# A grouped 1x1 convolution over 262144 pixels: two shared pieces in place of the 32-row piece

## The chip, the cores and the metric

The kernel runs on one core of a Trainium2 chip. The metric is the device time of one execution in microseconds; lower is better. The core has 16 DMA engines, which all of its transfers share.

## The reference

```python
# x: (1, 512, 512, 192) bf16, w: (1, 1, 4, 48, 48) bf16; G = 4 groups of Cg = 48 channels, k = 1
xg = xp.reshape(B, H, W, G, Cg)
out = out + jnp.einsum('bhwgc,gcd->bhwgd', xg, w[0, 0])
return out.reshape(B, H, W, C)
```

Every pixel's 192 channels are four groups of 48, and each group is multiplied by a 48 x 48 matrix of its own. All of x (100.66 MB) is read once, and an output of the same size is written.

## The kernel before, in words

**Layout.** A ring in SBUF, `ring`, has 128 rows (partitions) of 520 columns; a column is one pixel of 192 bf16 values, 384 bytes, in each row. It is divided into 5 places of 104 columns. A *piece* is a stretch of pixels that is loaded into one place, computed in the place (the output overwrites the input) and stored from it. A full piece of n columns takes 128 x n consecutive pixels, n to a row.

**Order.** `plan_pieces` lays the pieces out in *slots*, 0 to 20; slot s lies in place s mod 5. Slot 0 holds the head, three small pieces of 8, 20 and 32 columns. Nineteen slots hold a full piece of 104 columns (`BIG`). Slot 10 holds the *32-row piece* (`NARROW`): 48 columns, but only in rows 0 to 15 and 32 to 47. Its two blocks of 16 rows are transfers whose DRAM side is written with an outer dimension of 4 (`transfers`, lines 107 to 115), and each runs on four DMA engines, four rows on each; a full piece runs on all 16, eight rows on each. Pixels: 128 x (60 + 19 x 104) + 32 x 48 = 262144.

**Loads** are issued by SyncE (queue q1 of the profile), in the order of the pieces (line 175). Before it loads slot s it waits until all stores of slot s - 5 have landed.

**Compute** goes by *groups* of four columns, 521 in all: 15 in the head, 26 in a full piece, 12 in the 32-row piece, which takes as long per group as a full one. Two groups are a pair. TensorE transposes a group's 128 x 768 values in six 128 x 128 blocks (line 203) into PSUM, VectorE copies a pair to SBUF (line 242), TensorE multiplies by the weights (line 218), and ScalarE copies the result from PSUM into the ring (line 260). TensorE waits for a piece's load at that piece's first group. The semaphore `fa_done` counts ScalarE's copies.

**Stores** are issued by ScalarE (queue q10), between its copies, as soon as the copies of a piece, or of a part of it, are counted in `fa_done` (line 254). The pieces of slots 15 to 19 are stored in two halves of 52 columns (`LATE_PARTS`), the last in parts of 32, 32, 24 and 16 columns (`LAST_PARTS`).

GpSimd builds two constant tiles in the first 2 us and then does nothing more.

Of the kernel before, what the change touches and what calls it, by code (L numbers as in the profile page):

```python
# [6 lines left out]
BF16 = mybir.dt.bfloat16  # L7
# [4 lines left out]
C = GROUPS * CG  # L12
# [11 lines left out]

BIG = 104
RCOLS = 5 * BIG
HEAD = (8, 20, 32)
LATE = 6
LATE_PARTS = (52, 52)
LAST_PARTS = (32, 32, 24, 16)  # L30
FULL = ((0, 128),)
NARROW = ((0, 16), (32, 16))
NARROW_COLS = 48
NARROW_AT = (9,)
NXP = 4
NXS = 3
NOB = 4
# [2 lines left out]
class Waiter:  # L40

    def __init__(self, eng):
        self.eng = eng
        self.seen = {}
# [5 lines left out]
        self.eng.wait_ge(sem, val)  # L50


class Piece:

    def __init__(self, i, slot, at, g0, size, blocks, pix):
        self.i, self.slot, self.at, self.size = i, slot, at, size
        self.g0, self.g1 = g0, g0 + size // 4
        self.full = blocks is FULL
        self.blocks = []
        for (r0, rows) in blocks:  # L60
            self.blocks.append((r0, rows, pix))
            pix += rows * size
        self.pix_end = pix
        assert size % 4 == 0 and self.at + size <= RCOLS


def plan_pieces(npix):
    few = NARROW_COLS * sum(rows for _, rows in NARROW)
    at = [i for i in NARROW_AT if npix >= len(NARROW_AT) * few + 128 * (sum(HEAD) + BIG * (i + 2))]
    cols = (npix - few * len(at)) // 128  # L70
    assert cols % 4 == 0
    head = list(HEAD) if cols >= sum(HEAD) + BIG else []
    mid = cols - sum(head)
    slots = [[(BIG, FULL)]] * (mid // BIG) + ([[(mid % BIG, FULL)]] if mid % BIG else [])
    for i in at:
        slots.insert(i, [(NARROW_COLS, NARROW)])
    if head:
        slots.insert(0, [(s, FULL) for s in head])
    pieces, g, pix = [], 0, 0
    for n, parts in enumerate(slots):  # L80
        c = n * BIG % RCOLS
        for s, blocks in parts:
            pieces.append(Piece(len(pieces), n, c, g, s, blocks, pix))
            c, g, pix = c + s, pieces[-1].g1, pieces[-1].pix_end
    assert pix == npix
    return pieces


def bass_standalone__grouped__vision_kernel(nc, x, w, out):
    B, H, W_, Cx = x.shape  # L90
    assert Cx == C and tuple(w.shape) == (1, 1, GROUPS, CG, CG)
    npix = B * H * W_
    assert npix % 512 == 0, "the pixel count must be a multiple of 512"

    pieces = plan_pieces(npix)
# [4 lines left out]
    xf = x.rearrange("b h w c -> (b h w) c")  # L100
    of = out.rearrange("b h w c -> (b h w) c")
# [2 lines left out]
    def groups(pair):  # L104
        return range(2 * pair, min(2 * pair + 2, NG))

    def transfers(ap, ring, p, c0=0, c1=None):
        c1 = c1 or p.size
        for (r0, rows, pix) in p.blocks:
            px = ap[pix:pix + rows * p.size, :]  # L110
            if p.full:
                view = px.rearrange("(p i) n -> p (i n)", p=rows)[:, c0 * C:c1 * C]
            else:
                view = px.rearrange("(c a i) n -> a c (i n)", a=4, c=rows // 4)
            yield view, ring[r0:r0 + rows, (p.at + c0) * C:(p.at + c1) * C]

    stores = []
    for p in pieces:
        late = pieces[-1].slot - p.slot
        parts = LAST_PARTS if late == 0 else LATE_PARTS if late < LATE else (BIG,)  # L120
        c = 0
        for n in parts if p.size == BIG and p.full else (p.size,):
            stores.append((p, c, c + n, p.g0 + (c + n) // 4))
            c += n
    st_val = {p: 16 * sum(len(p.blocks) for q, *_ in stores if q is p) for p in pieces}

    with ExitStack() as es:
        block = es.enter_context(nc.Block())
# [9 lines left out]
        def sem(name):  # L138
            return es.enter_context(nc.semaphore(name))

        ld_sem = [sem(f"ld{p.i}") for p in pieces]
        st_sem = [sem(f"st{p.i}") for p in pieces]
        w_sem, id_sem, e_sem, wb_sem, wc_sem = (sem(s) for s in ("w_sem", "id_sem", "e_sem", "wb_sem", "wc_sem"))
        p0_sem, p1_sem = sem("p0_sem"), sem("p1_sem")
        t_done, mm_done = sem("t_done"), sem("mm_done")
        e_done, fa_done = sem("e_done"), sem("fa_done")

        def columns(g):
            p = piece_of[g]
            at = p.at + 4 * (g - p.g0)  # L150
            return ring[:, at * C:(at + 4) * C]

        @block.gpsimd
        def _(gp):
            gp.memset(esel[:], 1.0).then_inc(p0_sem, 1)  # L155
            gp.memset(ident[:], 1.0).then_inc(p1_sem, 1)  # L156
            gp.wait_ge(p0_sem, 1)
            gp.affine_select(out=esel[:], in_=esel[:], pattern=[[-1, ECOLS]],  # L158
                             compare_op=AluOpType.is_equal, fill=0.0, base=ESHIFT,
                             channel_multiplier=1).then_inc(e_sem, 1)  # L160
            gp.wait_ge(p1_sem, 1)
            gp.affine_select(out=ident[:], in_=ident[:], pattern=[[-1, 128]],  # L162
                             compare_op=AluOpType.is_equal, fill=0.0, base=0,
                             channel_multiplier=1).then_inc(id_sem, 1)

        @block.sync
        def _(sp):
            wq = Waiter(sp)
            sp.dma_start(w_sb[:], wv).then_inc(w_sem, 16)  # L169
            for p in pieces:  # L170
                for q in pieces:
                    if q.slot == p.slot - RCOLS // BIG:
                        wq.wait(st_sem[q.i], st_val[q])
                for dram, sbuf in transfers(xf, ring, p):
                    sp.dma_start(sbuf, dram).then_inc(ld_sem[p.i], 16)  # L175

        @block.tensor
        def _(pe):
            wq = Waiter(pe)

            def build_weights():
                wq.wait(e_sem, 1)
                wq.wait(w_sem, 16)
                last = None
                for (tc, r, g, c0_) in WBLOCKS:
                    s0 = ESHIFT - r
                    col = WOFF[tc] + c0_
                    last = pe.matmul(o_ps[:, NOB - 1, col:col + CG], lhsT=esel[:, s0:s0 + 128],  # L188
                                     rhs=w_sb[:, g, :], start=True, stop=True, skip_group_check=True)
                last.then_inc(wb_sem, 1)  # L190

            def transposes(pair):
                wq.wait(e_done, pair - 1)
                last = None
                for g in groups(pair):
                    p = piece_of[g]
                    if g == p.g0:
                        wq.wait(ld_sem[p.i], 16 * len(p.blocks))
                    xg = columns(g)
                    for ul in range(2):  # L200
                        for tc in range(3):
                            j = ul * 3 + tc
                            last = pe.transpose(xT_ps[:, g % NXP, j * 128:(j + 1) * 128],  # L203
                                                xg[:, j * 128:(j + 1) * 128], ident[:])
                last.then_inc(t_done, 1)

            def matmuls(pair):
                wq.wait(e_done, pair + 1)
                for g in groups(pair):
                    xs = xT_sb[pair % NXS][:, g % 2 * 2 * UC:(g % 2 + 1) * 2 * UC]  # L210
                    wq.wait(fa_done, g - 1)
                    last = None
                    for ul in range(2):
                        v = 2 * g + ul
                        for tc in range(3):
                            j = ul * 3 + tc
                            c0_, c1_ = COLR[tc]
                            last = pe.matmul(o_ps[:, v % NOB, c0_:c1_], lhsT=xs[:, j * 128:(j + 1) * 128],  # L218
                                             rhs=wt[:, WOFF[tc]:WOFF[tc] + (c1_ - c0_)],
                                             start=(tc == 0), stop=(tc == 2), skip_group_check=True)  # L220
                    last.then_inc(mm_done, 1)

            build_weights()
            wq.wait(id_sem, 1)
            transposes(0)
            wq.wait(wc_sem, 1)
            for pair in range(NP):
                if pair + 1 < NP:
                    transposes(pair + 1)
                matmuls(pair)  # L230
# [14 lines left out]
        @block.scalar  # L245
        def _(act):
            wq = Waiter(act)
            todo = list(stores)

            def store():  # L250
                p, c0, c1, g1 = todo.pop(0)
                wq.wait(fa_done, g1)
                for dram, sbuf in transfers(of, ring, p, c0, c1):
                    act.dma_start(dram, sbuf).then_inc(st_sem[p.i], 16)  # L254

            for g in range(NG):
                wq.wait(mm_done, g + 1)
                v = 2 * g
                dst = columns(g).rearrange("p (u c) -> p u c", u=2)
                act.copy(dst, o_ps[:, v % NOB:v % NOB + 2, 0:UC]).then_inc(fa_done, 1)  # L260
                while todo and todo[0][3] <= g:
                    store()
            while todo:
                store()
            for p in pieces:
                wq.wait(st_sem[p.i], st_val[p])
# [28 lines left out]
```

## Time and profile before

| | |
|---|---|
| runs | 485.15, 485.40, 485.44 us, median 485.4 |
| span of the profiled execution, first to last instruction | 483.3 us, 2.1 us under the median; its time with what lies around the span isn't listed separately |
| mean granted TensorE clock | 0.961 |
| moved by DMA | 202.23 MB in 7834 packets, mean 418 GB/s |
| TensorE waiting for loads | 21.1 us, 8 waits |
| SyncE's queue waiting for stores to land | 342.7 us in 15 waits, and 56.1 in one |
| issues | 25 loads of the ring and weights by SyncE, 32 stores by ScalarE, none by GpSimd |

How to read it: the page gives busy times of the compute engines, a row on the DMA engines by 40 slices of the span (the mean over the 16), and a part on the DMA queues. A queue isn't an engine: each transfer of q1 or q10 is spread over up to 16 engines, and every engine serves the packets of all queues. A packet is one row of a piece here, 39936 bytes for 104 columns; after its last row of a transfer an engine writes a semaphore, a packet of 4 bytes. q8 and q14 carry instructions that the core's engines fetch while they run, in packets of 16384 and 8192 bytes.

### The profile page before, as it was taken

To read this page: it belongs to the slowest core of one execution; us is meant where nothing else is said; L and a number is where in the kernel's file an instruction comes from. 1 tells how busy PE (TensorE), PEld (TensorE's weight loads), DVE (VectorE), ACT (ScalarE), POOL (GpSimd) and SP (SyncE) were. 2 spreads that over 40 slices of the span, in tenths; PEclk is the share of its full clock that TensorE was granted. 3 is DMA by queue.
4 is the path that set the end of the run, shared out by engine and by line. 5 is a ranking of instruction groups with operands and counts; after the bars stand their busy time and mean duration, and the time that the engine had idled before them with its cause. 6 is when DMAs were issued, how large, how long until landed. Compare 5 with 4: busy or idle time off the path is not lost.

```text
span 483.3 us, 13933 instructions
## 1 busy us (share of the span) xinstructions
PE 431.3 (89%) x6262; PEld 392.1 (81%) x6262; DVE 250.2 (52%) x262; ACT 392.6 (81%) x522; POOL 1.3 (0%) x8
## 2 busy tenths in 40 slices
PE   5699999999999999998599999979998999999910
PEld 5599888898898889887588988969787898899800
DVE  2345655656555565564256555544554655556500
ACT  2669999999999999998299999877888999999920
POOL 1000000000000000000000000000000000000000
PEclk9979999999999999999799999998999999999965
DMA  8999999999999999999999999999999999999993
GB/s 351 431 406 421 449 425 421 422 424 442 434 428 419 425 420 439 425 434 424 431 434 437 424 431 428 432 431 426 434 428 428 430 424 422 439 416 427 429 390 156
DMA packets 7834, 202.23 MB, mean 418 GB/s; under 512 B 1056, under 2 KB 1056, under 8 KB 1696
## 3 DMA queue, kind: packets, MB, share of 16 engines
q10 hardware_dynamic: 4360, 100.67, 48.7%
q1 hardware_dynamic: 3416, 100.68, 48.7%
q8 instruction: 50, 0.82, 0.6%
q14 instruction: 8, 0.07, 0.0%
HBM read 100.68 MB, written 100.66 MB: 417 GB/s over the span
## 4 chain that ended last, share of the span: by engine, by line
PE 54%; DMA 39%; ACT 1%; issue 1%; SPq 0%; ACTq 0%
PE o_ps L218 31%; PE xT_ps L203 22%; DMA ring<-in_x_dram 20%; DMA out_dram<-ring 19%; ACT ring L260 1%; SPq L175 0%; ACTq L254 0%; SPq L169 0%
## 5 line engine op out<-in xcount | busy, mean ns | idle before, releaser
L260 ACT CAST ring<-o_ps 128x768 bf16<-128x768 f32 x521 | 391.3, 802 | 68.5 <-PE o_ps L218 61.0
L242 DVE COPY xT_sb<-xT_ps 128x1536 bf16<-128x1536 bf16 (+1 forms) x261 | 249.6, 956 | 206.0 <-PE xT_ps L203 206.0
L218 PE MATMUL o_ps<-wt,xT_sb 128*128 128x144 bf16 (+1 forms) x3126 | 292.0, 236 | 5.9 <-ACT ring L260 1.3
L218 PEld LDWEIGHTS o_ps<-wt,xT_sb 128*128 128x128 bf16 x3126 | 212.0, 99 | 43.4 <-ACT ring L260 30.2
L203 PE MATMUL xT_ps<-ident,ring 128*128 128x128 bf16 x3126 | 222.7, 221 | 21.1 <-DMA ring<-in_x_dram 21.1
L203 PEld LDWEIGHTS xT_ps<-ident,ring 128*128 128x128 bf16 x3126 | 191.1, 99 | 22.7 <-DMA ring<-in_x_dram 19.8
L188 PE MATMUL o_ps<-w_sb,esel 48*128 48x48 bf16 x10 | 0.6, 210 | 2.7 <-DMA w_sb<-in_w_dram 2.7
L188 PEld LDWEIGHTS o_ps<-w_sb,esel 48*128 48x128 bf16 x10 | 0.5, 113 | 2.6 <-POOL esel L158 2.6
L236 DVE CAST wt<-o_ps 128x480 bf16<-128x480 f32 x1 | 0.7, 658 | 3.3 <-PE o_ps L188 3.3
L260 ACT ACT_TABLE_LOAD x1 | 1.3, 1283 | 0.8 <-PEq L280 0.8
L158 POOL TENSOR_SCALAR_AFFINE_SELECT esel<-esel 48x272 bf16<-48x272 bf16 x1 | 0.4, 405 | 0.0
L155 POOL MEMSET esel<- 48x272 bf16 x1 | 0.3, 318 | 0.3 <-POOLq L280 0.3
L162 POOL TENSOR_SCALAR_AFFINE_SELECT ident<-ident 128x128 bf16<-128x128 bf16 x1 | 0.3, 285 | 0.0
L156 POOL MEMSET ident<- 128x128 bf16 x1 | 0.2, 198 | 0.0
L280 POOL MEMSET const-bfloat16-1.0<- 128x1 bf16 x1 | 0.1, 102 | 0.0
L280 POOL MEMSET const-uint8-127<- 128x1 uint8 x1 | 0.1, 102 | 0.0
L280 POOL MEMSET const-float32-0.0<- 128x1 f32 x1 | 0.1, 98 | 0.3 <-issue 0.3
L280 POOL MEMSET const-float32-1.0<- 128x1 f32 x1 | 0.1, 98 | 0.0
## 6 DMA issues: line engine op xcount, KB each, us to landing
ring<-in_x_dram SPq DMA_DIRECT2D x19, 4992.0 KB, 37.5
out_dram<-ring ACTq DMA_DIRECT2D x13, 4992.0 KB, 45.5
out_dram<-ring ACTq DMA_DIRECT2D x10, 2496.0 KB, 47.7
out_dram<-ring ACTq DMA_DIRECT2D x3, 1536.0 KB, 19.7
ring<-in_x_dram SPq DMA_DIRECT2D x1, 1536.0 KB, 8.4
out_dram<-ring ACTq DMA_DIRECT2D x1, 1152.0 KB, 16.6
ring<-in_x_dram SPq DMA_DIRECT2D x1, 960.0 KB, 5.2
out_dram<-ring ACTq DMA_DIRECT2D x1, 960.0 KB, 28.6
```

The source lines that it names most:

```text
L155: gp.memset(esel[:], 1.0).then_inc(p0_sem, 1)
L156: gp.memset(ident[:], 1.0).then_inc(p1_sem, 1)
L158: gp.affine_select(out=esel[:], in_=esel[:], pattern=[[-1, ECOLS]], compare_op=AluOpType.is_equal, fill=0.0, base=ESHIFT, channel_multipli ...
L162: gp.affine_select(out=ident[:], in_=ident[:], pattern=[[-1, 128]], compare_op=AluOpType.is_equal, fill=0.0, base=0, channel_multiplier=1) ...
L188: last = pe.matmul(o_ps[:, NOB - 1, col:col + CG], lhsT=esel[:, s0:s0 + 128], rhs=w_sb[:, g, :], start=True, stop=True, skip_group_check=True)
L203: last = pe.transpose(xT_ps[:, g % NXP, j * 128:(j + 1) * 128], xg[:, j * 128:(j + 1) * 128], ident[:])
L218: last = pe.matmul(o_ps[:, v % NOB, c0_:c1_], lhsT=xs[:, j * 128:(j + 1) * 128], rhs=wt[:, WOFF[tc]:WOFF[tc] + (c1_ - c0_)], start=(tc == ...
L236: dve.tensor_copy(wt[:], o_ps[:, NOB - 1, 0:WCOLS]).then_inc(wc_sem, 1)
L242: dve.tensor_copy(xT_sb[pair % NXS][:, 0:n * 2 * UC].rearrange("p (g c) -> p g c", g=n), xT_ps[:, b0:b0 + n, 0:2 * UC]).then_inc(e_done, 1)
L260: act.copy(dst, o_ps[:, v % NOB:v % NOB + 2, 0:UC]).then_inc(fa_done, 1)
L280: nc = _bacc.Bacc("TRN2", target_bir_lowering=False, num_devices=1)
```

## The change

The 32-row piece goes, and with it one of the full pieces. Two *shared* pieces come, in slots 6 and 12. Each is three blocks of rows that start in the same column:

| rows | columns | rows to an engine | engines | issued by |
|---|---|---|---|---|
| 0 to 31 | 41 | 4 | 8 | SyncE (load), ScalarE (store) |
| 32 to 47 | 72 | 4 | 4 | SyncE, ScalarE |
| 52 to 95 | 72 | 4 | 11 | GpSimd, both |

The head has four pieces, 8, 20, 28 and 32 columns. Pixels: 128 x (88 + 18 x 104) + 2 x (32 x 41 + 16 x 72 + 44 x 72) = 262144. There are 526 groups: 22 in the head, 18 x 26, and 18 in each shared piece.

GpSimd issues ahead of each of its four data transfers a small one, 5 rows of 2 x 64 bytes from x into a tile `cur` that nobody reads (`CURSOR = 5`). The description of the change puts the data transfers on the 11 engines from engine 5 on; the small one is to move the point from which GpSimd's queue counts its engines by five. GpSimd waits for the place as SyncE does, loads, waits for the piece's copies in `fa_done`, stores, and goes on to the next shared piece. TensorE waits for both loads of a shared piece, SyncE for both stores before it loads into that place again.

```diff
-HEAD = (8, 20, 32)
+HEAD = (8, 20, 28, 32)
...
-FULL = ((0, 128),)
-NARROW = ((0, 16), (32, 16))
-NARROW_COLS = 48
-NARROW_AT = (9,)
+SHARED_AT = (5, 11)
+SHARED_COLS = 72
+SYNC, POOL = 0, 1
+SHARED = ((0, 32, 8, 41, SYNC), (32, 16, 4, SHARED_COLS, SYNC), (52, 44, 11, SHARED_COLS, POOL))
+CURSOR = 5
...
+    def transfers(ap, ring, p, queue, c0=0, c1=None):
+        for b in p.on(queue):
+            px = ap[b.pix:b.pix + b.rows * b.cols, :]
+            e0, e1 = c0, min(c1 or b.cols, b.cols)
+            if b.parts == 1:
+                view = px.rearrange("(p i) n -> p (i n)", p=b.rows)[:, e0 * C:e1 * C]
             else:
-                view = px.rearrange("(c a i) n -> a c (i n)", a=4, c=rows // 4)
-            yield view, ring[r0:r0 + rows, (p.at + c0) * C:(p.at + c1) * C]
+                view = px.rearrange("(c a i) n -> a c (i n)", a=b.parts, c=b.rows // b.parts)
+            yield view, ring[b.r0:b.r0 + b.rows, (p.at + e0) * C:(p.at + e1) * C]
...
+        def wait_slot(wq, p):
+            for q in pieces:
+                if q.slot == p.slot - RCOLS // BIG:
+                    wq.wait(st_sem[q.i], st_val[q])
+                    if q in pl_sem:
+                        wq.wait(ps_sem[q], pool_val[q])
...
+            turns = [0]
+
+            def pool_dmas(p, ap, inward, done):
+                for dram, sbuf in transfers(ap, ring, p, POOL):
+                    n = turns[0]
+                    few = xf[0:CURSOR, 0:128].rearrange("p (a b) -> p a b", a=2)[:, :, 0:32]
+                    gp.dma_start(cur[:, n], few).then_inc(cur_sem, 16)
+                    turns[0] += 1
+                    gp.dma_start(*((sbuf, dram) if inward else (dram, sbuf))).then_inc(done, 16)
+
+            for p in pooled:
+                wait_slot(wq, p)
+                pool_dmas(p, xf, True, pl_sem[p])
+                wq.wait(fa_done, p.g1)
+                pool_dmas(p, of, False, ps_sem[p])
+            for p in pooled:
+                wq.wait(ps_sem[p], pool_val[p])
+            wq.wait(cur_sem, 16 * turns[0])
...
-                        wq.wait(ld_sem[p.i], 16 * len(p.blocks))
+                        wq.wait(ld_sem[p.i], 16 * len(p.on(SYNC)))
+                        if p in pl_sem:
+                            wq.wait(pl_sem[p], pool_val[p])
```

More of the change, by code (lines that the diff above doesn't have):

```diff
@@ L50, in wait, with __init__, on @@
         self.eng.wait_ge(sem, val)
+class Block:
+    def __init__(self, r0, rows, parts, cols, queue, pix):
+        self.r0, self.rows, self.parts, self.cols, self.queue, self.pix = r0, rows, parts, cols, queue, pix
 class Piece:
-    def __init__(self, i, slot, at, g0, size, blocks, pix):
+    def __init__(self, i, slot, at, g0, size, shares, pix):
         self.i, self.slot, self.at, self.size = i, slot, at, size
         self.g0, self.g1 = g0, g0 + size // 4
-        self.full = blocks is FULL
+        self.full = shares is None
         self.blocks = []
-        for (r0, rows) in blocks:
-            self.blocks.append((r0, rows, pix))
-            pix += rows * size
+        for (r0, rows, parts, cols, queue) in shares or ((0, 128, 1, size, SYNC),):
+            self.blocks.append(Block(r0, rows, parts, cols, queue, pix))
+            pix += rows * cols
         self.pix_end = pix
         assert size % 4 == 0 and self.at + size <= RCOLS
+    def on(self, queue):
+        return [b for b in self.blocks if b.queue == queue]
 def plan_pieces(npix):
-    few = NARROW_COLS * sum(rows for _, rows in NARROW)
-    at = [i for i in NARROW_AT if npix >= len(NARROW_AT) * few + 128 * (sum(HEAD) + BIG * (i + 2))]
+    few = sum(rows * cols for _, rows, _, cols, _ in SHARED)
+    at = list(SHARED_AT)
+    if npix < len(at) * few + 128 * (sum(HEAD) + BIG * (at[-1] + 2)):
+        at = []
     cols = (npix - few * len(at)) // 128
@@ L73, in plan_pieces @@
     mid = cols - sum(head)
-    slots = [[(BIG, FULL)]] * (mid // BIG) + ([[(mid % BIG, FULL)]] if mid % BIG else [])
+    slots = [[(BIG, None)]] * (mid // BIG) + ([[(mid % BIG, None)]] if mid % BIG else [])
     for i in at:
-        slots.insert(i, [(NARROW_COLS, NARROW)])
+        slots.insert(i, [(SHARED_COLS, SHARED)])
     if head:
-        slots.insert(0, [(s, FULL) for s in head])
+        slots.insert(0, [(s, None) for s in head])
     pieces, g, pix = [], 0, 0
@@ L81, in plan_pieces @@
         c = n * BIG % RCOLS
-        for s, blocks in parts:
-            pieces.append(Piece(len(pieces), n, c, g, s, blocks, pix))
+        for s, shares in parts:
+            pieces.append(Piece(len(pieces), n, c, g, s, shares, pix))
             c, g, pix = c + s, pieces[-1].g1, pieces[-1].pix_end
@@ L105, in groups @@
         return range(2 * pair, min(2 * pair + 2, NG))
[L107 to L112, printed above, removed]
-            else:
-                view = px.rearrange("(c a i) n -> a c (i n)", a=4, c=rows // 4)
-            yield view, ring[r0:r0 + rows, (p.at + c0) * C:(p.at + c1) * C]
+    def transfers(ap, ring, p, queue, c0=0, c1=None):
[4 more added lines that the diff above has]
+                view = px.rearrange("(p i) n -> p (i n)", p=b.rows)[:, e0 * C:e1 * C]
+            else:
+                view = px.rearrange("(c a i) n -> a c (i n)", a=b.parts, c=b.rows // b.parts)
+            yield view, ring[b.r0:b.r0 + b.rows, (p.at + e0) * C:(p.at + e1) * C]
     stores = []
@@ L124, in bass_standalone__grouped__vision_kernel @@
             c += n
-    st_val = {p: 16 * sum(len(p.blocks) for q, *_ in stores if q is p) for p in pieces}
+    st_val = {p: 16 * sum(len(p.on(SYNC)) for q, *_ in stores if q is p) for p in pieces}
+    pooled = [p for p in pieces if p.on(POOL)]
+    pool_val = {p: 16 * len(p.on(POOL)) for p in pooled}
     with ExitStack() as es:
@@ L142, in bass_standalone__grouped__vision_kernel @@
         st_sem = [sem(f"st{p.i}") for p in pieces]
+        pl_sem = {p: sem(f"pl{p.i}") for p in pooled}
+        ps_sem = {p: sem(f"ps{p.i}") for p in pooled}
+        cur_sem = sem("cur_sem")
+        cur = es.enter_context(nc.sbuf_tensor("cur", [CURSOR, 2 * len(pooled), 2, 32], BF16))
         w_sem, id_sem, e_sem, wb_sem, wc_sem = (sem(s) for s in ("w_sem", "id_sem", "e_sem", "wb_sem", "wc_sem"))
@@ L151, in columns @@
             return ring[:, at * C:(at + 4) * C]
+        def wait_slot(wq, p):
[4 more added lines that the diff above has]
+                        wq.wait(ps_sem[q], pool_val[q])
         @block.gpsimd
         def _(gp):
+            wq = Waiter(gp)
             gp.memset(esel[:], 1.0).then_inc(p0_sem, 1)
@@ L170, in _ @@
             for p in pieces:
[L171 to L174, printed above, removed]
+                wait_slot(wq, p)
+                for dram, sbuf in transfers(xf, ring, p, SYNC):
                     sp.dma_start(sbuf, dram).then_inc(ld_sem[p.i], 16)
@@ L252, in store @@
                 wq.wait(fa_done, g1)
-                for dram, sbuf in transfers(of, ring, p, c0, c1):
+                for dram, sbuf in transfers(of, ring, p, SYNC, c0, c1):
                     act.dma_start(dram, sbuf).then_inc(st_sem[p.i], 16)
```

## The prediction

> **What bounds the kernel now.** I read the page's first three parts, then the table of busy time by stretch over the end of the span, then the waits, and last the records of single DMA packets.
>
> ```profile
> span 483.3 us, 13933 instructions
> ...
> PE 431.3 (89%) x6262; PEld 392.1 (81%) x6262; DVE 250.2 (52%) x262; ACT 392.6 (81%) x522; POOL 1.3 (0%) x8
> ...
> DMA  8999999999999999999999999999999999999993
> ...
> q10 hardware_dynamic: 4360, 100.67, 48.7%
> q1 hardware_dynamic: 3416, 100.68, 48.7%
> q8 instruction: 50, 0.82, 0.6%
> q14 instruction: 8, 0.07, 0.0%
> ```
>
> Loads (q1) and stores (q10) fill 97.4% of all 16 DMA engines' time, against 89% for PE. Only the last digit of the DMA row is low, so I cut the end into stretches (columns: PE, PEld, DVE, ACT, POOL busy, clock, DMA share, GB/s):
>
> ```profile
> 240.00:460.00 220.00, 209.60 (x3072) 190.00 (x3072) 122.68 (x129) 192.63 (x257) 0.00 (x0) 0.99 1.00 429
> 460.00:466.00 6.00, 0.69 (x8) 0.40 (x6) 0.00 (x0) 1.82 (x3) 0.00 (x0) 0.74 1.00 426
> 466.00:474.00 8.00, 0.00 (x0) 0.00 (x0) 0.00 (x0) 0.00 (x0) 0.00 (x0) 0.50 0.80 342
> 474.00:477.50 3.50, 0.00 (x0) 0.00 (x0) 0.00 (x0) 0.00 (x0) 0.00 (x0) 0.50 0.47 196
> 477.50:481.00 3.50, 0.00 (x0) 0.00 (x0) 0.00 (x0) 0.00 (x0) 0.00 (x0) 0.50 0.14 61
> 481.00:483.30 2.30, 0.00 (x0) 0.00 (x0) 0.00 (x0) 0.00 (x0) 0.00 (x0) 0.50 0.03 13
> ```
>
> Until 466 us every engine is busy all the time, whatever PE waits for. Then they drop out: 0.80 is 13 of 16, and at the end one works alone. Compute is over by then:
>
> ```profile
> PE xT_ps L203 <- DMA ring<-in_x_dram: 21.1, 8, 6.8
> ...
> 461.90 0.34 ACTq L254 DMA_DIRECT2D out_dram<-ring  x1
> ```
>
> The last store is issued at 461.9, 20 us before the last packet ends. So the time is that of the DMA engine with the most work, and PE's 21.1 us of waiting for loads is a result of it.
>
> Which engine that is, the packet records tell. They carry no engine number, but a busy engine starts its next packet 3 ns before the last one ends, and must serve the eight row packets and one semaphore write of every transfer in order; by these two rules the packets fall into 16 chains:
>
> ```
> engines  bytes each   instruction fetches          last packet ends, us
> 3        12.509 MB    none                         466.2 466.4 466.6
> 8        12.509 MB    q8, 6 or 7 each              474.2 474.6 474.6 475.1 475.1 475.6 475.9 476.6
> 4        12.804 MB    q14, 4 each on two of them   477.3 477.5 479.4 480.5
> 1        12.509 MB    none                         482.4
> ```
>
> The four with more bytes are those of the 32-row piece (they alone carry 18432-byte packets). The eight pay 50 fetches of 0.98 us, each with 0.33 us more for the packet behind it: 6.25 x 1.31 = 8.2 us. The last one, "the slow one", has no extra work: its 39936-byte stores take a median 1594 ns where all others take 1476, only while the compute engines run, 17.7 us in all. Why isn't shown. The mean of the 16 ends is 474.9: balance is worth at most 482.4 - 474.9 = 7.5 us.
>
> **The change, part by part.** A row packet of 104 pixels costs 1473 ns, so a pixel costs an engine 2 x 1473 / 104 = 28.3 ns, in and out. Pixels per engine, from the code: before, 2036 full columns x 8 rows = 16288 for all, and 48 x 8 = 384 more for four engines. After, 1960 full columns give 15680, and two shared pieces add: engines 0 to 3 get 2 x (4 x 41 + 4 x 72) = 904; engine 4 gets 2 x 4 x 41 = 328; engines 5 to 7 get 2 x (164 + 288) = 904; engines 8 to 15 get 2 x 288 = 576. If 0 to 3 are the four of the 32-row piece, 4 the slow one, 5 to 7 the three that end first and 8 to 15 those that fetch:
>
> - 0 to 3: 16672 to 16584, -2.5 us: 474.8, 475.0, 476.9, 478.0.
> - 4: 16288 to 16008, -7.9 us and 0.3 of its slow stores (17.7 x 280 / 16288): 474.1.
> - 5 to 7: 16288 to 16584, +8.4 us: 474.6 to 475.0.
> - 8 to 15: 16288 to 16256, -0.9 us: 473.2 to 475.7.
>
> The last end goes from 482.4 to 478.0, -4.4 us. The span ends 0.9 us after the last packet, so 478.9; the median of the runs, 485.4, lies 2.1 us above the profiled span, so 481.0.
>
> What else the change touches:
>
> - Compute: 521 groups become 526 (22 + 18 x 26 + 2 x 18). A group takes 0.81 us (172 copies in the 140 us from 80 to 220), so +4.1 us. The stores still queued hide it: with balance every engine has work up to about 474, and the last store, then issued at 466.0, is 8 packets of 231 ns on an engine, 1.8 us. Only if compute ended later than about 472 would that cover be gone; from there each us costs one.
> - Issues: two more on SP and two on ACT at 0.34 to 0.5 us. ACT is busy 128.6 us of the same 140 and has room for the 0.7; SP mostly waits. At nothing.
> - GpSimd: its 8 DMAs (four data, four small ones that move the queue's engine cursor by five) run on an engine that is idle after 2 us. Behind its wait for a slot and for the ACT copies stand only its own transfers.
> - New waits: PE waits for GpSimd's load ahead of a shared piece's first transposes; behind it is queued all of PE. In before slot 1's stores, which free slot 6's place, land by 84 us and PE reaches slot 6 at about 136 (its stores are issued at 157.5, 26 groups x 0.81 later). After, 7 groups more stand ahead: 142. In these 58 us GpSimd's 4 packets an engine need 4 x (1.02 + 2 x 1.48) = 16 us if three queues alternate. SP waits for GpSimd's store of slot 6 before it loads slot 11; behind it stand all later loads, and PE in the end. Before's slot 6 store, issued at 157.5, landed at 201.0 (the chain has it as 43.46 us of DMA), so 43 us is what SP waits anyway, against some 16 in GpSimd's queue. Both waits at nothing.
> - Cost of a packet in GpSimd's queue: not in the trace. Engines 5 to 15 get 4 rows x 2 pieces x 2 directions = 16 each. Lower bound: at line rate like the piece's 18432-byte packets (686 ns, all 64 alike), or 0 extra; a gain is excluded, no packet ran faster. Upper bound: like the other queue of foreign packets, q8, whose 16384 bytes cost 1.31 us against 0.60 at line rate, 0.7 more: 16 x 0.7 = 11 us. I take near 0.1 us, since the nearest row is the data packet: 1.6 us, which brings 8 to 15 to 477.3, still under 478.0.
> - The small cursor DMAs: 128 bytes a row. The 96-byte packets of the weight load took 9 to 211 ns; 4 x 2 of them cost an engine of 0 to 4 at most 1.7 us, probably 0.1.
>
> [...]
>
> **The rivals.**
>
> 1. GpSimd's packets fall on other engines than meant, so the change doesn't do what it says. For: nothing in the trace shows this queue's choice. With three rows each on 15 engines, 0 to 3 hold 2 x (164 + 288 + 216) more: 17016, +344 x 28.3 ns = +9.7 on the 480.5 engine, 490.2, time 493.3. With a cursor that starts elsewhere some of 0 to 3 hold 288 a piece: +13.8, time 497. Against: the four-engine blocks do sit on four engines exactly. It decides from 1.9 us, 66 pixels, on the latest of the four. Chance 0.08. [...]
> 2. The slow engine is one of 5 to 7: it gets 296 pixels instead of losing 280. 482.4 + 8.4 + 0.3 = 491.1, time 494.1, slower by 8.7. The records can't exclude it. That it and the three early ones are neighbours, they hint at: when the first store came, all four took its packets a round late (17.3 to 17.6 us), three of the piece's four and five of the fetching ones a round earlier (15.7 to 16.1). That it is the first of the four, only this: their first load packets start at 2.32 (the slow one), 2.37, 2.56 and 2.68 us. Chance 0.09. [...]
> 3. GpSimd's packets are dear. The engines that fetch have 482.4 - 475.7 = 6.7 us of room over 16 packets: from 0.42 us extra a packet the kernel is slower; at 0.7 they end at 487, time 490. For: q8's price. Against: every data packet's flat price. Chance 0.08, half of it past the point.
> 4. Nothing measurable: the slow engine is among the eight, and loses only 0.9 us. Chance 0.02.
>
> **How the numbers follow.** The forecast, all four groups as assumed, has 0.73: 481.0, its own range 478.0 (perfect balance, 474.9 + 0.9 + 2.1) to 484 (a few us for queue and cursor, or a slow engine that is less slow in unprofiled runs: then 480.5 to 478.0, -2.5). To reach 0.8 the range goes up to 487, into rival 3's cheaper half. What a measurement of this kernel can tell from no change is about 0.2%, 1 us. Faster: 0.73 + 0.02 of rival 3 = 0.75; same: 0.02 + 0.01 of rival 3 = 0.03; slower: 0.08 + 0.09 + 0.05 = 0.22.
>
> **What would show it.** Part 3 of the page gets a third data queue with 2 x 3168 pixels x 384 bytes each way, 4.9 MB in all. The DMA share stays 1.00 to about 473 and then falls within 5 us instead of 16; GB/s of the whole span rises to 422. All 16 chains end between 473 and 478.5, the last a q14 one of 0 to 3. Packets of 27648 bytes take 1.02 to 1.1 us on eleven engines. A chain that ends past 485 alone, or a store median of 1594 ns on an engine with 904 shared pixels, proves rival 1 or 2; 27648-byte packets over 1.4 us, rival 3. The last ACT issue past 474 would make compute the end, and my sum wrong.

## The result and the profile after

The changed kernel takes 486.8 us (median of six runs, 486.6 to 487.2) against 485.3 of the kernel before: a ratio of 1.003, 95% interval 1.0019 to 1.0042. It is slower by 1.5 us; the forecast was 4.4 us faster. First the page of the changed kernel, the lines that answer to those of before:

```profile
span 485.0 us, 14084 instructions
PE 436.1 (90%) x6322; PEld 397.3 (82%) x6322; DVE 252.6 (52%) x264; ACT 396.6 (82%) x527; POOL 5.9 (1%) x16
DMA  8999999999999999999999999999999999999993
q1 hardware_dynamic: 3496, 98.25, 47.6%
q10 hardware_dynamic: 4440, 98.23, 47.6%
q0 software_dynamic: 448, 4.87, 2.4%
q8 instruction: 50, 0.82, 0.6%
q14 instruction: 9, 0.07, 0.0%
```

The third data queue, q0, moves the 4.9 MB that the code says, and the span is 1.7 us longer. Then the end, in the stretches used before (the last one now goes on to 485):

```profile
240.00:460.00 220.00, 209.37 (x3069) 190.67 (x3070) 122.42 (x128) 191.81 (x257) 1.10 (x2) 0.98 1.00 425
460.00:466.00 6.00, 2.37 (x30) 1.69 (x27) 0.96 (x1) 3.56 (x5) 0.00 (x0) 0.84 1.00 427
466.00:474.00 8.00, 0.00 (x0) 0.00 (x0) 0.00 (x0) 0.00 (x0) 0.00 (x0) 0.50 0.97 413
474.00:477.50 3.50, 0.00 (x0) 0.00 (x0) 0.00 (x0) 0.00 (x0) 0.00 (x0) 0.50 0.59 248
477.50:481.00 3.50, 0.00 (x0) 0.00 (x0) 0.00 (x0) 0.00 (x0) 0.00 (x0) 0.50 0.24 104
481.00:485.00 4.00, 0.00 (x0) 0.00 (x0) 0.00 (x0) 0.00 (x0) 0.00 (x0) 0.50 0.13 54
```

From 466 to 474 us the share is 0.97 where it was 0.80: the three engines that had dropped out have work now, as planned. But between 477.5 and 481 it is 0.24, four engines of 16, and they go on to 482.4 to 483.9. Before, the share there was 0.14, and one engine went on to 482.4. The end is one of DMA as before: PE's waits for loads shrank from 21.1 to 14.2 us in total, and the last store is issued 20 us before the end (the waits, then the last line of ScalarE's timeline):

```profile
PE xT_ps L247 <- DMA ring<-in_x_dram: 14.2, 5, 5.0
```

```profile
463.86 0.34 ACTq L298 DMA_DIRECT2D out_dram<-ring  x1
```

The packet records, put into chains by the two rules of the prediction, say which engines the four are. The engine numbers come from the first experiment. After its last shared packet engine 4 has the same packets as 8 and 15; of these three chains the one with the slow stores is taken for engine 4.

```
engines   instruction fetches   last packet ends, us
                                before           forecast         after
0, 2      none                  477.2 477.5      474.8 475.0      476.4 476.5
1, 3      q14                   479.4 480.5      476.9 478.0      482.4 483.4
4         none (slow stores)    482.4            474.1            477.5
5, 6      q8                    474.2 to 476.6   474.6 to 475.0   483.3 483.9
7         none                  466.2 to 466.6   474.6 to 475.0   475.2
8, 15     none                  466.2 to 466.6   473.2 to 475.7   472.0 472.2
9 to 14   q8                    474.2 to 476.6   473.2 to 475.7   474.4 to 477.1
mean                            474.9            474.9            477.3
```

Two of the three engines that were to have spare time, 5 and 6, had none: they fetch instructions. Engines 1 and 3 end 5.4 us later than forecast, and the mean engine 2.4 us later.

### The profile page after: what moved, and what is told of

Read it like the earlier page. It is cut to its first block, busy times and chain, and to the rows that moved or that the text cites. A ratio compares the mean times of both kernels' runs of the same rounds, so it can differ in the third digit from the quotient of the medians.

```text
span 485.0 us, 14084 instructions
## 1 busy us (share of the span) xinstructions
PE 436.1 (90%) x6322; PEld 397.3 (82%) x6322; DVE 252.6 (52%) x264; ACT 396.6 (82%) x527; POOL 5.9 (1%) x16
## 4 chain that ended last, share of the span: by engine, by line
PE 70%; DMA 22%; issue 1%; another core or an unknown queue 1%; ACT 1%; ACTq 0%; SPq 0%
PE o_ps L262 41%; PE xT_ps L247 29%; DMA ring<-in_x_dram 13%; DMA out_dram<-ring 9%; ACT ring L304 1%; ACTq L298 0%; SPq L217 0%; SPq L213 0%
## 5 line engine op out<-in xcount | busy, mean ns | idle before, releaser
L304 ACT CAST ring<-o_ps 128x768 bf16<-128x768 f32 x526 | 395.3, 802 | 66.4 <-PE o_ps L262 57.4
L286 DVE COPY xT_sb<-xT_ps 128x1536 bf16<-128x1536 bf16 x263 | 252.0, 958 | 205.3 <-PE xT_ps L247 205.3
L262 PE MATMUL o_ps<-wt,xT_sb 128*128 128x144 bf16 (+1 forms) x3156 | 295.6, 236 | 9.7 <-ACT ring L304 3.9
L262 PEld LDWEIGHTS o_ps<-wt,xT_sb 128*128 128x128 bf16 x3156 | 214.6, 99 | 47.2 <-ACT ring L304 33.7
L247 PE MATMUL xT_ps<-ident,ring 128*128 128x128 bf16 x3156 | 224.6, 222 | 14.3 <-DMA ring<-in_x_dram 14.2
L247 PEld LDWEIGHTS xT_ps<-ident,ring 128*128 128x128 bf16 x3156 | 193.7, 99 | 15.5 <-DMA ring<-in_x_dram 12.5
L197 POOL DMA_DIRECT2D cur<-in_x_dram x4 | 2.3, 584 | 286.3 <-DMA out_dram<-ring 160.0
L199 POOL DMA_DIRECT2D ring<-in_x_dram x2 | 1.1, 564 | 0.0
L199 POOL DMA_DIRECT2D out_dram<-ring x2 | 1.1, 559 | 0.0
```

Of the source, the lines that this page charges most:

```text
L197: gp.dma_start(cur[:, n], few).then_inc(cur_sem, 16)
L199: gp.dma_start(*((sbuf, dram) if inward else (dram, sbuf))).then_inc(done, 16)
L286: dve.tensor_copy(xT_sb[pair % NXS][:, 0:n * 2 * UC].rearrange("p (g c) -> p g c", g=n), xT_ps[:, b0:b0 + n, 0:2 * UC]).then_inc(e_done, 1)
```

## The experiments

The main theory (A): engines 5 and 6 are among the eight that fetch instructions, and the 8.4 us that the change gives to each come on top. Its rivals: (B) GpSimd's queue costs time, by its packets or by its turns; (C) the extra packet time of single engines is chance; (G, D) the new cut of the pieces makes packets slow; (Q, E) the queue or the shared pieces do. "Excess" below is the time that the 39936-byte packets take above 1473 ns each, summed over all 16 engines, from the packet records.

**Which number each engine has.** 45 tiny loads of 1 to 15 rows are issued behind three of the loads; an engine's number is 15 less the count of those that have a packet in its chain, out of one set of 15. That a load of n rows runs on engines 0 to n - 1 is assumed; no record carries a number.

```diff
+LABEL_AT = (4, 13, 19)
...
+                if p.slot in LABEL_AT:
...
+                    for n in range(1, 16):
...
+                        sp.dma_start(lab[0:n, n - 1, off:off + few], xf[0:n, 0:few]).then_inc(lab_sem, 16)
```

> The kernel before, with 45 tiny loads that number the DMA engines: three times (behind the loads of slots 4, 13 and 19) SyncE issues 15 loads of 1, 2, ... 15 rows of 32, 28 or 24 bytes; a load of n rows should run on engines 0 to n-1, so an engine's number is 15 less the number of its packets. Theory A (the step that put the fetching engines at 8 to 15 was wrong): the slow engine, with stores of about 1594 ns, is engine 4, and two of engines 5 to 7 carry six or seven q8 fetches each; two of engines 8 to 15 carry none. Rival B (the map was right, GpSimd's queue slows others): 5 to 7 carry no fetch, all of 8 to 15 do. Time: 486 to 490 us, the labels being 360 packets of some 0.1 us or less and 45 issues of 0.4 us on SyncE.

> The changed kernel with the same 45 loads. Theory A: the same two of engines 5 to 7 fetch and end last, near 483.5 us, and so do the two of engines 0 to 3 with q14 fetches if their extra store time of the profile after (4 to 5 us each) comes again; engine 4 near 477, GpSimd's 27648-byte packets on 5 to 15 at 1025 ns. Rival B: the engines that end last differ from those, and carry GpSimd's packets without fetching. Rival C (the extra store time on single engines between 265 and 306 us is chance): it is absent or elsewhere, and the two that fetch end alone. Time 487 to 491 us.

The kernel before with the labels took 488.8 us, the changed kernel 492.8 (one execution each), so the labels cost 4 to 6 us and the times are of no use. The map is. The load queue's line of the labelled kernel before:

```profile
q1 hardware_dynamic: 4136, 100.69, 48.6%
```

That is 720 packets more than the 3416 of before: 3 x 120 rows and as many semaphore writes, and 120 is 15 + 14 + ... + 1, so a load of n rows has one packet on each of n engines. By the counts a chain holds, the four engines of the 32-row piece are 0 to 3, the slow one is 4, the q8 fetches fall on 5, 6 and 9 to 14, five to seven each, the q14 fetches on 1 and 3, and the three engines without any that end first are 7, 8 and 15. The changed kernel gives the same map. Theory A's premise holds: of "5 to 7" only 7 had spare time.

**GpSimd's queue by itself.** The kernel before with the full pieces of slots 6 and 12 loaded and stored by GpSimd, on all 16 engines; balance is as before.

```diff
+POOL_SLOTS = (6, 12)
...
+            for p in pooled:
...
+                    gp.dma_start(sbuf, dram).then_inc(ld_sem[p.i], 16)
+                wq.wait(fa_done, p.g1)
...
+                    gp.dma_start(dram, sbuf).then_inc(st_sem[p.i], 16)
...
```

> The kernel before, with the full pieces of slots 6 and 12 loaded and stored by GpSimd's queue (8 rows to each of 16 engines, 4 DMAs), all else as before: every engine's work is that of before, only the queue differs. Theory A: no change beyond 0.5 us (485.3). Rival B (GpSimd's queue costs the engines time): slower by 1 to 5 us, as the sum of the extra packet times in the profile after has it.

488.0 us, ratio 1.0057 (1.0044 to 1.0069). The typical packet is not dear: 512 of 39936 bytes in this queue have a median of 1476 ns, that of the other queues. But the DMA engines stand idle at one place. Its stretch from 260 to 280 us:

```profile
260.00:280.00 20.00, 19.78 (x298) 18.04 (x296) 11.81 (x13) 18.40 (x25) 0.00 (x0) 1.00 0.84 330
```

and the same stretch of the kernel before:

```profile
260.00:280.00 20.00, 19.79 (x298) 18.03 (x296) 11.48 (x12) 18.41 (x25) 0.00 (x0) 1.00 0.99 425
```

By the packet records 57 engine-us are idle there, 3.6 us for each of 16 engines on average, until the load that SyncE issues at 272.7 us. That is near the 2.8 us that were lost, and yet not where the time goes: the engine that ends last, the slow one, has no gap there and ends 2.7 us later than before. What grew on it is packet time, an excess of 16.7 us against 14.3. On all engines the excess is 112.5 engine-us against 62.1, with 62.5 against 12.7 from 240 to 340 us. So rival B holds in part: two full pieces in GpSimd's queue, without any shared piece, bring slow packets in all queues. Why isn't shown. The idle place itself isn't the changed kernel's loss: there the stretch from 240 to 460 us stays at 1.00.

**The changed kernel once more,** without an edit, to see whether the same places are disturbed again.

> The changed kernel once more, with a profile. Theory A: 486.8 us; the two engines with 12.737 MB and q8 fetches end at 483 to 484 us as in the first profile. Rival C: the extra time of 3 to 5 us on two of engines 0 to 3 (265 to 306 us) and the round of slow packets of all engines near 89 us stand at other times or are gone.

486.8 us, ratio 1.0031 (1.002 to 1.0042). The four late engines are the same: 482.5 and 483.2 (1 and 3), 483.8 and 484.4 (5 and 6). The excess is 93.3 engine-us (90.5 in the first profile, 62.1 before), with 4.5 to 15 engine-us in each 20 us from 60 to 100 and from 260 to 340 us in both (2.2 to 4.0 before). The extra packet time comes at the same places in both profiles of this program, so rival C falls.

**Engines 5 and 6 relieved.** GpSimd's block goes to engines 7 to 15, with more columns.

```diff
-SHARED_COLS = 72
+SHARED_COLS = 88
-SHARED = ((0, 32, 8, 41, SYNC), (32, 16, 4, SHARED_COLS, SYNC), (52, 44, 11, SHARED_COLS, POOL))
-CURSOR = 5
+SHARED = ((0, 32, 8, 41, SYNC), (32, 16, 4, 72, SYNC), (60, 36, 9, SHARED_COLS, POOL))
+CURSOR = 7
```

> The changed kernel with GpSimd's 44 x 72 pixels moved to rows 60 to 95, 88 columns, on engines 7 to 15: the same pixels through the same queue, but engines 5 and 6, which fetch instructions, lose 2 x 288 pixels, 16.3 us, and 7 to 15 gain 2 x 64, 3.6 us. Shared pieces are 88 columns wide, 8 groups more, 6.5 us of compute that the stores should still hide. Theory A (5 and 6 end the changed kernel at 483.3 to 484.4): they end at 467 to 468; the end passes to engines 1 and 3, at 482.4 to 483.3 if their extra store time stays, or to 9 to 14 at 478 to 481. Time 485.4, about 1.3 under the changed kernel, and as low as 482 if the extra store time of 1 and 3 goes. Rival B (GpSimd's queue costs what was lost): 486.8 or more, the queue has as much to move.

484.3 us, ratio 0.9988 (0.9973 to 1.0003): 2.5 us under the changed kernel, whose interval lies wholly above this one, and some 1 us under theory A's sum. Its end, and the stretch from 300 to 320 us:

```profile
300.00:320.00 20.00, 19.78 (x297) 18.00 (x295) 11.55 (x13) 18.41 (x26) 0.00 (x0) 1.00 0.94 402
```

```profile
474.00:477.50 3.50, 0.00 (x0) 0.00 (x0) 0.00 (x0) 0.00 (x0) 0.00 (x0) 0.50 0.79 333
477.50:481.00 3.50, 0.00 (x0) 0.00 (x0) 0.00 (x0) 0.00 (x0) 0.00 (x0) 0.50 0.30 126
481.00:485.00 4.00, 0.00 (x0) 0.00 (x0) 0.00 (x0) 0.00 (x0) 0.00 (x0) 0.59 0.00 2
```

Nothing works past 481.4, and the two that end there are 1 and 3. So 5 and 6 were the end of the changed kernel, and 1 and 3 stood close behind. The 2.5 us are not the effect of 5 and 6 alone: 1 and 3 also end some 2 us earlier than in the changed kernel, as they meet fewer slow packets (1.6 and 1.8 us above line rate, 1476 ns a packet, from 240 to 320 us, there 3.4 and 3.5). The 0.94 is a new loss, 18.8 engine-us: mostly engines 5 and 6, which had less to do and ran dry, and which the sum had not counted.

**All engines by the true map.** Of each shared piece 0 to 3 take 272 pixels each, 5 to 15 take 128 by GpSimd's queue, 7 and 8 another 160, and 4 nothing. The 72 columns left over go into slot 1, so the shared pieces lie in slots 7 and 13.

```diff
-HEAD = (8, 20, 28, 32)
+HEAD = (8, 20, 32)
...
-SHARED_AT = (5, 11)
+SHARED_AT = (6, 12)
...
-SHARED = ((0, 32, 8, 41, SYNC), (32, 16, 4, SHARED_COLS, SYNC), (52, 44, 11, SHARED_COLS, POOL))
-CURSOR = 5
+SHARED = ((0, 16, 4, 34, SYNC), (32, 16, 4, 34, SYNC),
+          (52, 44, 11, 32, POOL, 0, (5,)), (60, 8, 2, 40, POOL, 32, (7, 7)))
...
```

> The shares dealt out by the engine map: 2004 full columns for all; two shared pieces with 2 x 272 pixels to engines 0 to 3 (two blocks of 16 rows, 34 columns, SyncE and ScalarE), 2 x 128 to engines 5 to 15 (rows 52 to 95, 32 columns, GpSimd), 2 x 160 more to 7 and 8 (rows 60 to 67, 40 columns, GpSimd), none to 4. Head 8, 20, 32, then a full piece of 72 columns and 18 of 104. Theory A, from the ends of before and 28.3 ns a pixel: 0 and 2 at 474.7, 1 and 3 at 476.8 and 477.9, 4 at 474.5, the fetching 5, 6 and 9 to 14 at 474.5 to 477, 7 and 8 at 475.6, 15 at 466.5; last end 478, time 481. With the changed kernel's extra times (1 and 3 later by 5, 4 by 3): 483, time 486. Rival B (the queue costs the time): no gain, 486 or more, as GpSimd moves 3 DMAs each way a piece.

483.6 us (482.2 to 486.6), ratio 0.9971 (0.9954 to 0.9989): faster than both kernels, by 0.3% on the one before, and still 2.6 us over the sum.

```profile
466.00:474.00 8.00, 0.00 (x0) 0.00 (x0) 0.00 (x0) 0.00 (x0) 0.00 (x0) 0.50 0.99 421
474.00:477.50 3.50, 0.00 (x0) 0.00 (x0) 0.00 (x0) 0.00 (x0) 0.00 (x0) 0.50 0.64 267
477.50:481.00 3.50, 0.00 (x0) 0.00 (x0) 0.00 (x0) 0.00 (x0) 0.00 (x0) 0.50 0.09 40
```

This is nearly the shape that the prediction described for the changed kernel: full to 474, then down within 6 us; the last packet ends at 479.9, on engine 3. With the map right the idea gains 1.6 us. The profiled execution is one of the shorter ones, 482.6 us; in it the mean engine ends at 476.6, not 474.9, and that is what stays above the sum.

**The same, trimmed by the profile:** 0 to 3 take 224 pixels each, 5 to 15 take 144, and 7 and 8 another 168. The edit is against the version above.

```diff
-SHARED_COLS = 72
+SHARED_COLS = 80
...
-SHARED = ((0, 16, 4, 34, SYNC), (32, 16, 4, 34, SYNC),
-          (52, 44, 11, 32, POOL, 0, (5,)), (60, 8, 2, 40, POOL, 32, (7, 7)))
+SHARED = ((0, 16, 4, 28, SYNC), (32, 16, 4, 28, SYNC),
+          (52, 44, 11, 36, POOL, 0, (5,)), (60, 8, 2, 42, POOL, 36, (7, 7)))
```

> The rebalanced kernel with a little less on engines 0 to 3 (two blocks of 28 columns, -96 pixels, -2.7 us), a little more on 5 to 15 (36 columns, +32 pixels, +0.9 us) and on 7 and 8 (36 + 42 columns, +48 pixels, +1.4 us), shared pieces 80 columns wide. From the ends in the rebalanced kernel's profile (engines 1 and 3 at 478.7 and 479.9, the fetching ones 475 to 478, 7 and 8 at 476.6 and 477.2): last ends 477 to 479, time 481.5 to 482.5, against 483.6. Rival F (the stray slow packets of 250 to 340 us follow whichever engines run ahead): no gain, 483 to 486.

A miss: 487.2 us (483.7 to 490.5), ratio 1.0028 (1.0003 to 1.0053). The profiled execution, one of the longer ones at 490.4 us, has an excess of 100.3 engine-us (71.7 in the version above), 40 of it between 300 and 380 us (17.5 above), and the mean engine ends at 479. The two that end last, at 485.2 and 487.8, are 7 and 8: they got 48 pixels or 1.4 us more, and 4.9 and 6.6 us of slow stores, where the version above has under 1 us on each. Balance of a few pixels is worth less than what the packets' own times move.

**The head.** The changed kernel with the old head, and the 28 columns in slot 1 (shared pieces in slots 7 and 13).

```diff
-HEAD = (8, 20, 28, 32)
+HEAD = (8, 20, 32)
-SHARED_AT = (5, 11)
+SHARED_AT = (6, 12)
-    slots = [[(BIG, None)]] * (mid // BIG) + ([[(mid % BIG, None)]] if mid % BIG else [])
+    slots = ([[(mid % BIG, None)]] if mid % BIG else []) + [[(BIG, None)]] * (mid // BIG)
```

> The changed kernel with the head of before (8, 20, 32) and the 28 columns as a full piece of its own in the slot behind it (slots 1 to 21, shared pieces in slots 7 and 13). Shares, queues and pixels per engine are those of the changed kernel. In its profiles all 16 engines ran slow from 60 to 100 us (mean 39936-byte packet 1520 and 1547 ns against 1489 and 1492 in before and in the rebalanced kernel), about 1.5 us each. Theory D (that comes with the longer head and what it shifts): gone, all ends 1.5 us earlier, 5 and 6 last at 482 to 483, time 485.3. Theory E (it comes with the shares or GpSimd's queue): still there, 486.8. Theory A alone has 5 and 6 last in both cases.

488.0 us, ratio 1.0062 (1.0048 to 1.0075), so neither theory's time. The slow stretch from 60 to 100 us shrinks from 23.7 to 16.6 engine-us, another appears at 140 to 200 (21.9 against 7.3), and the excess is 90.8 as in the changed kernel. The end says more:

```profile
477.50:481.00 3.50, 0.00 (x0) 0.00 (x0) 0.00 (x0) 0.00 (x0) 0.00 (x0) 0.50 0.24 101
481.00:485.00 4.00, 0.00 (x0) 0.00 (x0) 0.00 (x0) 0.00 (x0) 0.00 (x0) 0.50 0.11 48
```

Past 481 two engines are left, 5 and 6, and they end at 484.5 and 485.0. Engines 1 and 3 end at 477.9 and 478.7, near the 476.9 and 478.0 of the prediction; here it is 0 and 2 that lose over 3 us each from 240 to 320 us, and they end at 479.9 and 480.2. So in this run the wrong map sets the time by itself, and which engines meet the late slow packets changes with the cut.

**The head in the kernel before,** with one full piece cut to 76 columns and no shared piece.

```diff
-HEAD = (8, 20, 32)
+HEAD = (8, 20, 28, 32)
...
+    slots.insert(5, [(mid % BIG, FULL)])
```

> The kernel before with the changed kernel's head (8, 20, 28, 32) and, in slot 6, a full piece of 76 columns for one of the 104; no shared piece, no GpSimd queue, every engine has the bytes it had. It asks where the changed kernel's extra packet time comes from: its 39936-byte packets spend 90.5 engine-us above 1473 ns each, against 62.1 before, 1.8 us more on the mean engine. Theory G (the cut of the pieces alone, which shifts which loads and stores run side by side, brings slow packets): 75 engine-us or more, with slow stretches between 60 and 100 us; time 486 to 487. Theory Q (the GpSimd queue or the shared pieces bring them): within 5 of 62 engine-us; time 485.2, within 0.5.

484.9 us, ratio 0.9993 (0.9984 to 1.0001). The stretch from 60 to 100 us, in this kernel

```profile
60.00:100.00 40.00, 38.75 (x579) 35.32 (x577) 22.79 (x25) 36.00 (x49) 0.00 (x0) 1.00 1.01 420
```

in the changed one

```profile
60.00:100.00 40.00, 39.56 (x594) 36.06 (x592) 23.17 (x25) 36.81 (x50) 1.26 (x2) 1.00 1.01 418
```

and in the kernel before:

```profile
60.00:100.00 40.00, 39.56 (x588) 35.97 (x587) 23.70 (x25) 36.64 (x49) 0.00 (x0) 1.00 1.00 429
```

With the new head the engines are just as busy and move 2% less: this slow stretch comes with the head (an excess of 25.4 engine-us in these 40 us, 23.7 in the changed kernel, 7.5 before). In this kernel it costs no time: other stretches are quieter, and the sum is 65.3 against 62.1. So the stretch alone doesn't make the miss.

**The shared pieces without GpSimd's queue.** Their third block goes to SyncE and ScalarE.

```diff
-SHARED = ((0, 32, 8, 41, SYNC), (32, 16, 4, SHARED_COLS, SYNC), (52, 44, 11, SHARED_COLS, POOL))
+SHARED = ((0, 32, 8, 41, SYNC), (32, 16, 4, SHARED_COLS, SYNC), (52, 44, 11, SHARED_COLS, SYNC))
```

> The changed kernel with the third block of its shared pieces (rows 52 to 95) loaded by SyncE and stored by ScalarE instead of GpSimd's queue; no small DMAs. By the map the block then lies on engines 0 to 10, so 0 to 4 carry 576 pixels more, 16.3 us: engines 1 and 3 end at 482.4 to 483.4 + 16.3 = 499 to 500, time about 502 by either theory. What is asked is the excess of the 39936-byte packets up to 340 us, where balance plays no part yet: theory Q, it falls to what the kernel before has there; theory G, it stays what the changed kernel has.

505.3 us, ratio 1.0417 (1.0394 to 1.044), 3 us over the sum. The excess up to 340 us is 150 engine-us; the changed kernel has 79, the one before 57. Without the third queue there are more slow packets, not fewer: with the shared pieces the queue isn't needed for them. The block lies on other engines here, so balance changed as well.

**The shared pieces later,** in slots 8 and 14.

```diff
-SHARED_AT = (5, 11)
+SHARED_AT = (7, 13)
```

> The changed kernel with its shared pieces in slots 8 and 14 instead of 6 and 12; each engine's bytes are the same. Theory G: the slow stretch of 60 to 100 us stays (nothing before it changed), the one of 260 to 340 us moves or changes, and the time is 486.8 within 2 us, since engines 5 and 6 still have 8.4 us of work more than before. Theory Q: the stretch of 260 to 340 us comes some 42 us later with the pieces, as the GpSimd store of slot 14 stands 52 groups behind that of slot 12; time the same 486.8.

488.3 us, ratio 1.0053 (1.0037 to 1.007), inside the band given. The early stretch stays (25.1 engine-us from 60 to 100). The late one begins some 40 us later: from 240 to 280 us it is 4.6 engine-us, 9.2 in the changed kernel, and from 320 to 380 us 23.7 against 15.9. So it comes with the shared pieces or with their transfers in GpSimd's queue, which move together here. The run above has slow packets without the queue, the one with two full pieces in it has them without shared pieces, so neither is needed for such a stretch. The end has the changed kernel's shape:

```profile
477.50:481.00 3.50, 0.00 (x0) 0.00 (x0) 0.00 (x0) 0.00 (x0) 0.00 (x0) 0.50 0.24 103
481.00:485.00 4.00, 0.00 (x0) 0.00 (x0) 0.00 (x0) 0.00 (x0) 0.00 (x0) 0.50 0.25 105
485.00:489.00 4.00, 0.00 (x0) 0.00 (x0) 0.00 (x0) 0.00 (x0) 0.00 (x0) 0.50 0.04 16
```

Again a quarter of the engines, four, work on alone: 5 and 6 to 485.2 and 485.7, 1 and 3 to 485.3 and 486.4.

## Why the prediction was wrong

**The step that failed** is the assumption that hands out the pixels: "5 to 7 the three that end first and 8 to 15 those that fetch". The line built on it, "5 to 7: 16288 to 16584, +8.4 us: 474.6 to 475.0", is right for engine 7 (475.2) and wrong for 5 and 6. They start from the ends of the fetching engines, 474.2 to 476.6, and the same + 8.4 gives 482.6 to 485.0; measured were 483.3 and 483.9. With 0.9 and 2.1 us behind it, the prediction's own arithmetic with the right map gives a time of 485.6 to 488.0, and 486.8 was measured. The labelled loads show the map. The run with 5 and 6 relieved is 2.5 us shorter, part of it from 1 and 3; in the run with the old head 5 and 6 end alone, at 484.5 and 485.0, within the same bounds.

**What was wrong in the reasoning** is the chance more than the arithmetic. The records before can't number the engines, as the prediction said. Three early engines among the 11 beyond the slow one can lie in 165 ways, and only one is 5, 6 and 7; the evidence for it was a difference of 1.5 us in when four engines took their first stores. That got 0.73. A rival "one or two of 5 to 7 fetch" was missing, though its price stood in the table, and its point of decision too: a single fetching engine with 8.4 us more ends after 482.4.

**A term that was mis-sized:** engines 1 and 3 were given -2.5 us and gained 3. Their 39936-byte packets take 3.4 and 3.5 us above line rate (1476 ns) between 240 and 320 us, where before they had 0.6 at most, and some 1 us between 80 and 120, where before they had 0.2; engines 8 and 15 lose about 5 us each between 240 and 360. The larger part is the late slow stretch. The prediction let the time of a packet stay as it was, and had no term for it. By itself it would have brought the end of this kernel to 483.4, so a right map alone would not have saved the forecast: with 5 and 6 relieved the time is 484.3, not 481. Why these engines are slowed stays open: the stretch begins later when the shared pieces come later, it falls on 0 and 2 with the old head, and two full pieces in GpSimd's queue bring such a stretch too. In the two-queue run balance is worst and the excess largest, 150 engine-us up to 340 us; whether the one brings the other isn't shown.

**Engine 4** was the slow one, as assumed (rival 2 is out), and ended 3.4 us later than its forecast. The runs don't take this apart.

**What held.** 28.3 ns a pixel, in and out: it puts engine 7, which got 296 pixels and has no fetches, within 0.2 us of its end, and 5 and 6 inside the bounds above. GpSimd's queue goes where the code means it to: its 27648-byte packets lie on exactly 11 chains, 16 on each, and engine 4 has none (rival 1 is out). They take a median of 1025 ns, as the 27648-byte packets of q1 and q10 do, and the cursor's 128-byte packets 13 ns (rival 3 is out). The 44 rows fell on 11 engines, 5 to 15 by the labels, four rows on each; three rows each on 15 engines, the first case of rival 1, no run shows. Compute stayed hidden: the last store is issued at 463.9, earlier than the 466.0 allowed for it. SyncE's waits for stores sum to 400 us (333 + 68) against 399 before, and PE's for loads fell, so the two new waits cost nothing. The median lies 1.8 us above the span, 2.1 was used.

**The signs that were named:** q0's 4.9 MB, packets of 1.02 us and compute off the end came. Those of balance did not: the chains end between 472.0 and 483.9, not 473 and 478.5, the DMA share is still 0.24 past 477.5, and the GB/s of the whole span are 417, not 422.

## What to carry to other kernels

To move work between single DMA engines, number them first: a few labelled loads of 1 to 15 rows cost 4 to 6 us in one run and tell which engine fetches, which is slow and which has time. An assumption about which engine is which gets the share of the arrangements that the records leave open, not the chance of its arithmetic. Where the whole gain is the gap between the last engine and the mean (7.5 us here), the mean must be forecast too: it moved by 2.4 us without a byte more. With the right map 1.6 of the 4.4 us were left, and after one more small edit none.

## What the hardware showed that was not expected

- Instruction fetches are not spread over all DMA engines in these kernels: the 50 of q8 (16384 bytes, 0.98 us in the kernel before, some 1.3 with what the next packet takes longer) fall on engines 5, 6 and 9 to 14 alone, those of q14 on 1 and 3.
- One engine, 4, has slow stores in every kernel that was taken apart (median 1578 to 1594 against 1476 ns), only while the compute engines run: in the kernel before, its 19968-byte stores fall from some 800 ns to the 742 of the others between 459 and 464 us, where compute ends. Why engine 4 is slow isn't shown.
- A queue of GpSimd's can run at line rate in the median packet (1476 ns) and still cost time: when two full pieces went through it, 57 engine-us were idle at one place, the excess on all queues rose by 50 engine-us, and the kernel took 2.8 us more.
- Stretches of slow packets come at the same times in both profiled executions of the changed kernel (in the first, 39936-byte packets of up to 2.78 us where the median is 1.48), and lie elsewhere when pieces move; an edit that adds no byte moves the mean engine's end by 0.7 us (the longer head) to 6.8 us (two full pieces in GpSimd's queue).
